# Fewer weight columns per level product, fixed PSUM tiles for the small products, and one instruction per sum of the state

## The chip, the cores and the metric

The kernel runs on 1 core of a Trainium2 chip. The metric is device time in microseconds (us): the median of the runs of one kernel. The kernel before took 584.26 us (median of 3 runs, 584.08 to 585.15).

## The reference, cut to what matters

An RWKV-6 recurrence (batch 4, 8 heads, 768 tokens, head dimension 48) feeds an expert layer of 2048 hidden units. Everything is fp32.

```python
for t in range(S):                       # S = 768
    cur   = einsum('bhd,bhe->bhde', u * k[t], v[t])
    y[t]  = einsum('bhd,bhde->bhe', r[t], state + cur)
    state = w[t][:, :, :, None] * state + einsum('bhd,bhe->bhde', k[t], v[t])
x = y.transpose(0, 2, 1, 3).reshape(3072, 384)
h = x @ w_in                             # 384 x 2048
g = h * erf(softplus(h))
out = g @ w_out                          # 2048 x 384
```

## The kernel before

**Steps.** The tokens are cut into 6 chunks of 128. A step `s` handles one chunk of two of the four batches, so there are 12 steps, 0 to 11. In a step stand 16 (batch, head) combinations, as 8 pairs `n` of two heads `e`. Head `e` of a pair has its 48 dimensions in partitions 64e to 64e+47 (`rows(e)`); partitions 48 to 63 and 112 to 127 are padding of zeros. A chunk is worked on as two halves of 64 tokens (`HC`).

**Level products.** Inside a half, what earlier tokens give to later ones is built up by levels 1 to 6. At level `l` the half is cut into blocks of 2^l tokens, and the later `half = 2^(l-1)` tokens of each block (queries r) meet its earlier `half` tokens (keys k). `level_products` (L540 to L556) does a level with 32 matmuls: for each pair, half and head, the key tokens are the weights (`lhsT`, one weight column per key token) and the query tokens of all right halves are the moving operand (32 columns; 64 at level 1). So the PSUM tile `pp` has key tokens in its partitions. `take_level` (L558) then copies from `pp` into `own` with `copy_predicated` (L562) only where a mask says that key and query belong to the two halves of one block. At levels 1 to 5 the weights are all 64 key tokens, at level 6 the first 32. Key tokens from 64 - `half` on lie in the last block's later half: no mask of levels 2 to 5 takes them. At level 1 the mask also holds the diagonal, so all 64 are needed there.

**Decay.** Between levels, `scale` (L328; L321 in step 0) multiplies the products of w into the tile `in` (r and k) in place, so a level waits for the `scale` of the level before, and that waits for the matmuls of its own level, which read `in`.

**Which levels run where.** Step 0 is `attend_first` (L746), steps 1 to 4 `attend` (L876), steps 5 to 11 `attend_late` (L693). Steps 0 to 3 run levels 1 to 6 on TensorE, step 4 levels 4 to 6, and steps 5 to 11 only levels 5 and 6: the nearer distances are there multiplied and summed up on VectorE and GpSimd (L453 to L484) and come back through DRAM as `by_tokens` (L514).

**State.** `state_part` (L650) multiplies keys and values of each half into PSUM, head 0 in partitions 0 to 47 and head 1 in 64 to 111. VectorE adds it to the faded state: `middle` after the first half (L736, L960, or a copy at L962), `S_next` after the second (L743, L965, L852); GpSimd fades `middle` in between (L739, L963). Each sum is a loop of two instructions, one for each head. `through_state` (L598, matmuls at L610) and `from_own` (L575, matmuls at L584) bring state and `own` into the output tile `y`.

**PSUM.** All small products share two tiles of 4 KB in each partition, `pp0` and `pp1`. Each call of `products` (L131) asks the pool for a new tile of that name, which may be used once everything that touched the one before it is released.

**The expert layer and the order.** `hidden` (L994, matmuls at L1027), `project` (L1044, L1059), `project_fast` (L1127, L1142) and `hidden_of_two` (L1210, L1230) do the two large products for earlier steps. The order on every engine is that of the code (a manual schedule): pieces of the expert layer are placed by hand between the levels (`place`, `beside`, and for the late steps lists of letters that `run_late` reads), so that TensorE has work while a level waits for VectorE. In step 0, where no such work exists yet, `keep_busy` (L867, matmuls at L871) and `stay_warm` (L858, matmuls at L862) put idle matmuls in the gaps. Steps 1 and 2 also turn the given weights into fp32 (L255 to L285).

The program names each matmul once; in the trace each fp32 matmul stands as two instructions, each with its own weight load, so that a level is 64 of them.

Of the kernel before, what the change touches and what calls it, by code (L numbers as in the profile page):

```python
# [11 lines left out]
FP32 = mybir.dt.float32  # L12
# [5 lines left out]
P = 128  # L18
FAST = 3
EP = 64  # L20
HC = 64
# [22 lines left out]
MASKED = 5  # L44
# [7 lines left out]
def rights(ap, half):  # L52

    names = "abcdefg"[: len(ap.shape) - 1]
    spread = " ".join(names)
    return ap.rearrange(f"{spread} (n two h) -> {spread} n two h", two=2, h=half)[
        (slice(None),) * len(names) + (slice(None), 1)
    ]
# [3 lines left out]
def kernel(  # L62
# [14 lines left out]
    nc = tc.nc  # L77
    PSUM = bass.MemoryType.PSUM

    n_steps, _, _, JP, C = rkw.shape  # L80
    NH, D = v.shape[2:]
    NP = JP // NJ
    NE = NH // JP
# [17 lines left out]
    ps_p = ctx.enter_context(tc.tile_pool(name="ps_p", bufs=1, space=PSUM))  # L101
# [7 lines left out]
    middle = const.tile([P, JP, D], FP32, name="middle")  # L109
    faded = [const.tile([P, JP, D], FP32, name="faded")] * NC  # L110
# [17 lines left out]

    turns = {"next": 0}

    def products(shape, n=None):  # L131


        if n is not None:
            return ps_p.tile(shape, FP32, name=f"pp{n}")
        n = turns["next"]
        turns["next"] = 1 - n
        return ps_p.tile(shape, FP32, name=f"pp{n}")

    loaded = {}  # L140

# [160 lines left out]

    def rows(e, n=D):
        return slice(e * EP, e * EP + n)

    def at(e, p):

        return rows(e ^ p & 1)
# [215 lines left out]
    def parts_of(s):  # L524

        c, i = divmod(s, SPC)
        in_t, vt = loaded[s]
        made, tots, tot = ready[s]
        ends = tot.rearrange("p (n h) -> p n h", h=NC)
        return c, in_t, vt, made, states[i][c % 2], states[i][1 - c % 2], ends  # L530

    def by_pair(t):

        return lambda x, n: t[:, x, n]
# [5 lines left out]
    def level_products(pp, rk, level, ns=range(NJ * NP)):  # L540

        half = 1 << (level - 1)
        m = HC if level <= MASKED else half
        for n in ns:
            for s0 in range(0, C, HC):
                for e in range(NE):
                    right = rk(0, n)[rows(e), s0 : s0 + HC]
                    to = pp[s0 : s0 + m, e, n, :]
                    if level > 1:
                        right = rights(right, half)  # L550
                        to = to[:, : HC // 2].rearrange("p (b h) -> p b h", h=half)
                    nc.tensor.matmul(  # L552
                        to, lhsT=rk(1, n)[rows(e), s0 : s0 + m], rhs=right,
                        start=True,
                        stop=True,
                    )  # L556

    def take_level(own, pp, level):  # L558
        half = 1 << (level - 1)
        got = pp[:].rearrange("p e n t -> p (e n) t")  # L560
        if level <= MASKED:
            nc.vector.copy_predicated(  # L562
                rights(own[:], half),
                rights(mask_sb[:, level - 1 : level, :].to_broadcast([P, NH, HC]), half),
                got[..., : HC // 2].rearrange("p n (b h) -> p n b h", h=half),
            )
        else:
            for s0 in range(0, C, HC):
                nc.scalar.copy(own[s0 : s0 + half, :, half:], got[s0 : s0 + half, :, :half])
# [5 lines left out]
    def from_own(s, own, swap):  # L575
        vt = loaded[s][1]
        for j in range(NJ):
            for q in range(0, NP, 2):
                for h in range(NC):
                    e = h ^ swap  # L580
                    for p in (q, q + 1):
                        n = j * NP + p
                        t = slice(h * HC, (h + 1) * HC)
                        nc.tensor.matmul(  # L584
                            y[at(e, p), e, p // 2, j, t],
                            lhsT=vt[t, n * NE + e, :], rhs=own[t, e * JP + n, :],
                            start=swap == 1 and not j and not q, stop=True,
                            skip_group_check=True,
                        )

    def fence():

        nc.vector.tensor_copy(
            out=seen[:].rearrange("p (e g t) -> p e g t", e=NE, g=NP),
            in_=y[:].rearrange("p e q j t -> p e (q j) t")[..., HC - 1 : HC + 1],
        )
# [96 lines left out]
    def attend_late(s, run):  # L693

        c, in_t, vt, own, S, S_next, ends = parts_of(s)
        RK = by_pair(in_t)
        before = s - 1 if s - 1 > DIRECT else None
        if before:
            from_own(before, ready[before][0], 1)
            fence()  # L700
        pp = products([P, NE, JP, HC], 0)
        level_products(pp, RK, LOG - 1)
        scale(s, LOG - 1)
        take_level(own, pp, LOG - 1)
        run("front", None)
        if before:
            from_own(before, ready[before][0], 0)
            through_state(before, xTs[before])
            if s + 1 < n_steps:
                load_step(s + 1)  # L710
        following = prepare(s + 1) if s + 1 < n_steps else iter(())
        next(following, None)
        nc.gpsimd.tensor_mul(faded[0][:], S[:], ends[:, :, 0:1].to_broadcast([P, JP, D]))
        next(following, None)
        run("near", None)
        next(following, None)
        kT = kTs[s]
        nc.vector.tensor_mul(
            kT[:].rearrange("p (e n) d -> p n e d", e=NE),
            kT[:].rearrange("p (e n) d -> p n e d", e=NE), spread[s][:],  # L720
        )
        run(0, following)

        pp = products([P, NE, JP, HC], 0)
        level_products(pp, RK, LOG)
        if s + 1 < n_steps:
            spread_blocks(s + 1, pp)
        take_level(own, pp, LOG)
        scale(s, LOG)
        run(1, following)  # L730
        ps = products([P, NC, JP, HC], 0)
        ps = [[ps[:, h]] * NE for h in range(NC)]
        state_part(s, kT, ps)
        run(2, following)
        for e in range(NE):
            nc.vector.tensor_add(middle[rows(e)], faded[0][rows(e)], ps[0][e][rows(e), :, :D])  # L736
        run(3, following)
        if s < n_steps - SPC:
            nc.gpsimd.tensor_mul(  # L739
                faded[1][:], middle[:], ends[:, :, 1:2].to_broadcast([P, JP, D])  # L740
            )
            for e in range(NE):
                nc.vector.tensor_add(S_next[rows(e)], faded[1][rows(e)], ps[1][e][rows(e), :, :D])  # L743
        run(4, following)

    def attend_first(xT):  # L746
# [5 lines left out]
        c, _, vt, made, S, S_next, ends = parts_of(0)  # L752
# [4 lines left out]
        pp = products([P, NE, JP, HC])  # L757
# [21 lines left out]
        for level in range(2, LOG):  # L779
            pp = turns.pop("pp", None) or products([P, NE, JP, HC])  # L780
# [21 lines left out]
        pp = turns.pop("pp")  # L802
# [29 lines left out]
        ps = [[products([P, NE, JP, HC], 1 - e)[:, e] for e in range(NE)]]  # L832
# [15 lines left out]
        def pending():  # L848
            part = products([P, NE, JP, HC], turns["next"])[:, 0]
            state_part(0, kT, ps + [[part] * NE], (1,))  # L850
            for e in range(NE):
                nc.vector.tensor_add(S_next[rows(e)], faded[1][rows(e)], part[rows(e), :, :D])  # L852
            load_third()
            stages["l"](5, S_next[:, 0, 0:1])

# [20 lines left out]
    def attend(s, xT, early, place, behind):  # L876

        c, in_t, vt, made, S, S_next, ends = parts_of(s)
# [9 lines left out]
        for level in range(near_log(s) + 1 if s == DIRECT else 1, LOG + 1):  # L888
            rk = by_pair(made) if level == 1 else RK
            pp = turns.pop("pp", None) or products([P, NE, JP, HC])  # L890
# [45 lines left out]
        ps = products([P, JP, P])  # L936
# [17 lines left out]
        ps = products([P, NC, JP, HC])  # L954
        ps = [[ps[:, h]] * NE for h in range(NC)]
        state_part(s, kT, ps)
        from_own(s, own, 0)
        for e in range(NE):
            if c:
                nc.vector.tensor_add(middle[rows(e)], faded[0][rows(e)], ps[0][e][rows(e), :, :D])  # L960
            else:
                nc.vector.tensor_copy(middle[rows(e)], ps[0][e][rows(e), :, :D])  # L962
        nc.gpsimd.tensor_mul(faded[1][:], middle[:], ends[:, :, 1:2].to_broadcast([P, JP, D]))  # L963
        for e in range(NE):
            nc.vector.tensor_add(S_next[rows(e)], faded[1][rows(e)], ps[1][e][rows(e), :, :D])  # L965
        for _ in following:
            pass
        place(LOG + 1)
# [433 lines left out]
    make_identity(nc, ident[:])  # L1402
    nc.vector.memset(y[:], 0.0)
    nc.vector.memset(sums[:], 0.0)
    apart = mixed[:].rearrange("p i f n -> p (i f n)")[:, : KT * P]
    apart = apart.rearrange("p (k m) -> p k m", k=KT)
    nc.vector.memset(apart, 0.0)
    for kk in range(KT):
        n = D // KT
# [187 lines left out]
```

## Time and profile before

| what | value |
|---|---|
| median of 3 runs | 584.26 us (584.08 to 585.15) |
| span of the profiled execution | 585.1 us, 0.84 above the median |
| granted TensorE clock, mean | 0.999 |
| TensorE matmuls (PE) busy | 576.4 us, 99% |
| weight loads (PEld) busy | 495.1 us, 85% |
| VectorE (DVE) busy | 454.7 us, 78%, 558 instructions |
| ScalarE (ACT), GpSimd (POOL) busy | 355.6 us, 274.1 us |
| L552, level products, weight loads of 64 columns, moving 32 | 1600 |
| L552, the same with weight loads of 32 columns (level 6) | 768 |
| L552, level 1, weight loads of 64 columns, moving 64 | 256 |
| sums of the state (L736, L743, L852, L960, L962, L965) | 42 instructions of 548 to 556 ns each |

How to read it: the span runs from the first to the last instruction of one execution on the chip. PE is busy while matmuls run, PEld while weights are loaded; the two overlap. A line like "x64" merges neighbouring instructions of one kind, and what stands in square brackets is how long the engine stood idle before them and what ended that. The chain of waits follows the work that ended last back to the start. The 1600 loads are 25 levels of 64: levels 2 to 5 in steps 0 to 3, levels 4 and 5 in step 4, level 5 in steps 5 to 11.

### The profile page before, as it was taken

The numbers are of one execution on the slowest core, as the hardware profiler recorded it, in microseconds if no ns is written. First come the engines' busy times: TensorE is split into PE (matmuls) and PEld (weight loads), VectorE is DVE, ScalarE is ACT, GpSimd is POOL, SyncE is SP. The second block draws the span as 40 slices with busy tenths as digits, with TensorE's granted clock in tenths as the row PEclk, the third lists the DMA queues.
The fourth block names the chain that finished last, engine by engine and source line by source line (L and its number), as shares of the span: only waits on it lengthen the run. The fifth ranks groups of instructions, "written<-read, shape, count | busy, mean of one in ns | idle before, by whom it ended". The sixth has DMA issues, their size and how long they took to land.

```text
span 585.1 us, 16663 instructions
## 1 busy us (share of the span) xinstructions
PE 576.4 (99%) x7240; PEld 495.1 (85%) x7240; DVE 454.7 (78%) x558; ACT 355.6 (61%) x478; POOL 274.1 (47%) x313
## 2 busy tenths in 40 slices
PE   8899999999999999999999999999999999999997
PEld 6588887688668758998898898898898899988997
DVE  6776886999996899799799799799799637256630
ACT  3658877644544598756766666665765771387700
POOL 4557391702398469659459459449549200000000
PEclk9999999999999999999999999999999999999999
DMA  8587571440433414334334334334331301000000
GB/s 269 177 273 281 201 235 44 183 154 10 145 95 116 117 55 156 63 116 165 74 111 169 74 108 172 75 108 136 74 108 55 74 8 36 2 0 2 28 27 29
DMA packets 54082, 63.25 MB, mean 108 GB/s; under 512 B 35160, under 2 KB 40568, under 8 KB 52984
## 3 DMA queue, kind: packets, MB, share of 16 engines
q1 hardware_dynamic: 53624, 61.98, 33.4%
q8 instruction: 57, 0.93, 0.6%
q10 hardware_dynamic: 384, 0.20, 0.1%
q14 instruction: 17, 0.14, 0.1%
HBM read 52.39 MB, written 8.69 MB: 104 GB/s over the span
## 4 chain that ended last, share of the span: by engine, by line
PE 95%; DVE 3%; issue 1%; ACT 0%; POOL 0%; DVEq 0%; POOLq 0%
PE m L1027 36%; PE m L1142 28%; PE m L1059 8%; PE pp L552 6%; PE pp L1230 4%; PE y L1230 2%; PE y L584 2%; PE pp L659 2%; PE y L610 2%; PE m L862 1%; PE pp L871 1%; PE pp L938 1%; DVE in L328 1%; DVE words L467 1%; PE pp L1142 0%
## 5 line engine op out<-in xcount | busy, mean ns | idle before, releaser
L1027 PE MATMUL m<-xT,w_in_sb 128*128 128x256 f32 x960 | 215.3, 382 | 0.1
L1027 PEld LDWEIGHTS m<-xT,w_in_sb 128*128 128x128 f32 x960 | 179.9, 190 | 26.2 <-issue 1.0
L328 DVE TENSOR_TENSOR in<-in,tot_sb 128x1024 f32<-128x1024 f32 (+1 forms) x55 | 75.3, 1369 | 16.5 <-PE pp L552 13.2
L463 POOL TENSOR_TENSOR rk<-words 128x528 f32<-128x528 f32 (+3 forms) x28 | 42.5, 1517 | 91.2 <-DVE sums L453 80.7
L1036 ACT COPY h<-m 128x512 f32<-128x512 f32 x80 | 46.4, 579 | 57.6 <-PE m L1027 57.5
L467 POOL TENSOR_TENSOR words<-words,rest 128x528 f32<-128x528 f32 (+10 forms) x77 | 78.1, 1015 | 6.0
L1059 PE MATMUL m<-w_out_sb,h 128*128 128x384 f32 x192 | 64.3, 491 | 0.0
L1059 PEld LDWEIGHTS m<-w_out_sb,h 128*128 128x128 f32 x192 | 35.7, 190 | 23.5
L1142 PE MATMUL m<-mixed,h 128*128 128x192 f32 x256 | 45.6, 331 | 0.0
L1142 PE MATMUL m<-w_out_sb,h 128*128 128x192 f32 x256 | 44.8, 329 | 0.0
L552 PEld LDWEIGHTS pp<-in 48*64 48x64 f32 (+1 forms) x2368 | 33.4, 126 | 12.0 <-issue 6.2
L1142 PEld LDWEIGHTS m<-mixed,h 128*128 128x128 f32 x256 | 41.4, 190 | 0.9
L1142 PEld LDWEIGHTS m<-w_out_sb,h 128*128 128x128 f32 x256 | 41.6, 190 | 0.3
L1142 PE MATMUL m<-w_out_sb,room 128*128 128x192 f32 x240 | 41.5, 326 | 0.0
L983 ACT ACT_TABLE_LOAD x30 | 38.5, 1283 | 2.7 <-issue 2.2
L987 ACT ACT_TABLE_LOAD x30 | 38.5, 1283 | 1.5 <-DVE room L1125 1.1
L1142 PEld LDWEIGHTS m<-w_out_sb,room 128*128 128x128 f32 x240 | 39.4, 190 | 0.0
L402 POOL TENSOR_TENSOR tot_sb<-tot_sb 128x256 f32<-128x256 f32 (+4 forms) x50 | 36.2, 724 | 3.8
L552 PE MATMUL pp<-in 48*64 48x32 f32 (+1 forms) x2368 | 37.3, 212 | 0.6 <-DVE in L328 0.5
L463 POOL TENSOR_TENSOR words<-words 128x336 f32<-128x336 f32 (+6 forms) x49 | 35.3, 720 | 3.8
L453 DVE TENSOR_REDUCE sums<-rk 128x14 f32<-128x672 f32 (+9 forms) x54 | 34.7, 701 | 0.0
L453 DVE TENSOR_REDUCE sums<-words 128x6 f32<-128x288 f32 (+8 forms) x66 | 26.9, 464 | 3.9 <-POOL words L463 3.6
(198 smaller groups left out, 951.5 us busy)
## 6 DMA issues: line engine op xcount, KB each, us to landing
in<-in_rkw SPq DMA_DIRECT2D x8, 1024.0 KB, 5.1
words<-in_moe_w_in SPq DMA_DIRECT2D x16, 384.0 KB, 5.4
words<-in_moe_w_out SPq DMA_DIRECT2D x16, 384.0 KB, 4.7
words<-in_rk_rows SPq DMA_DIRECT2D x8, 768.0 KB, 5.6
w<-in_rkw SPq DMA_DIRECT2D x11, 512.0 KB
v<-in_v SPq DMA_DIRECT2D x12, 384.0 KB, 5.6
out<-o SPq DMA_DIRECT2D x23, 192.0 KB, 2.4
in<-in_rkw SPq DMA_DIRECT2D x7, 512.0 KB, 5.7
```

Source lines behind the costliest of these rows:

```text
L328: nc.vector.tensor_mul(halves, halves, view(tots[level - 1], 0, [[1, n], [2, nb], [0, half]]))
L402: nc.gpsimd.tensor_mul(new, pair[:, :, 0], pair[:, :, 1])
L453: nc.vector.tensor_reduce(out=view(sums[:], n, [[near * (NEAR + 1), NEAR // near], [NEAR + 1, near - n]]), in_=terms[n], axis=mybir.AxisLi ...
L463: engine.tensor_mul(terms[n], r[:, :, n:], k[:, :, : near - n])
L467: engine.tensor_mul(k[:, :, :m], k[:, :, :m], w[:, :, n : n + m])
L552: nc.tensor.matmul(to, lhsT=rk(1, n)[rows(e), s0 : s0 + m], rhs=right, start=True, stop=True,)
L983: nc.scalar.activation(sp_room, chunks[0], AF.Softplus)
L987: nc.scalar.activation(at, sp_room, AF.Erf)
L1027: nc.tensor.matmul(ps[:, ff, :], lhsT=w_in_sb[:, g * FG + f + ff, kk * P : (kk + 1) * P], rhs=xT[:, kk, :], start=kk == 0, stop=kk == KT - 1,)
L1036: nc.scalar.copy(h[:, f : f + FT, :], ps[:])
L1059: nc.tensor.matmul(ps[j][:], lhsT=gs[g][:, f, j * C : (j + 1) * C], rhs=w_out_sb[:, g * FG + f, :], start=g + f == 0, stop=g == NG - 1 and ...
L1142: nc.tensor.matmul(to, lhsT=a[:, f], rhs=b[:, f], start=start and f == 0, stop=f == FG - 1, skip_group_check=True,)
```

## The change

Three edits, none of which moves an instruction to another place in the order.

1. At levels 2 to 5 the weights are the first 64 - `half` key tokens: 62, 60, 56 and 48 columns at levels 2, 3, 4 and 5. Level 1 keeps 64, level 6 keeps 32.
2. `products` no longer asks the pool: two tiles `banks` are taken once, set to zero by VectorE at the start (two memsets of 128x1024), and every product is a view of one of them. The rows that a level now leaves unwritten keep what was there.
3. Each sum of the state is one instruction over partitions 0 to 111 (`both`) in place of two over 48 partitions each; the padding in between is summed with it and never read.

```diff
+    banks = [ps_p.tile([P, NE * JP * HC], FP32, name=f"pp{n}") for n in range(2)]
+
     def products(shape, n=None):
-        if n is not None:
-            return ps_p.tile(shape, FP32, name=f"pp{n}")
-        n = turns["next"]
-        turns["next"] = 1 - n
-        return ps_p.tile(shape, FP32, name=f"pp{n}")
+        if n is None:
+            n = turns["next"]
+            turns["next"] = 1 - n
+        names = "abc"[: len(shape) - 1]
+        return banks[n][:].rearrange(
+            f"p ({' '.join(names)}) -> p {' '.join(names)}", **dict(zip(names, shape[1:]))
+        )
...
+    both = slice(0, EP + D)
...
     def level_products(pp, rk, level, ns=range(NJ * NP)):
         half = 1 << (level - 1)
-        m = HC if level <= MASKED else half
+        m = HC - half if 1 < level <= MASKED else HC if level == 1 else half
...
     # attend_late; the same in attend (with the copy at its first chunk) and in pending()
-        for e in range(NE):
-            nc.vector.tensor_add(middle[rows(e)], faded[0][rows(e)], ps[0][e][rows(e), :, :D])
+        nc.vector.tensor_add(middle[both], faded[0][both], ps[0][0][both, :, :D])
...
-            for e in range(NE):
-                nc.vector.tensor_add(S_next[rows(e)], faded[1][rows(e)], ps[1][e][rows(e), :, :D])
+            nc.vector.tensor_add(S_next[both], faded[1][both], ps[1][0][both, :, :D])
...
     nc.vector.memset(sums[:], 0.0)
+    for t in banks:
+        nc.vector.memset(t[:], 0.0)
```

More of the change, by code (lines that the diff above doesn't have):

```diff
@@ L850, in pending @@
             state_part(0, kT, ps + [[part] * NE], (1,))
-            for e in range(NE):
-                nc.vector.tensor_add(S_next[rows(e)], faded[1][rows(e)], part[rows(e), :, :D])
+            nc.vector.tensor_add(S_next[both], faded[1][both], part[both, :, :D])
             load_third()
@@ L957, in attend @@
         from_own(s, own, 0)
[L958 to L962, printed above, removed]
+        if c:
+            nc.vector.tensor_add(middle[both], faded[0][both], ps[0][0][both, :, :D])
+        else:
+            nc.vector.tensor_copy(middle[both], ps[0][0][both, :, :D])
         nc.gpsimd.tensor_mul(faded[1][:], middle[:], ends[:, :, 1:2].to_broadcast([P, JP, D]))
-        for e in range(NE):
-            nc.vector.tensor_add(S_next[rows(e)], faded[1][rows(e)], ps[1][e][rows(e), :, :D])
+        nc.vector.tensor_add(S_next[both], faded[1][both], ps[1][0][both, :, :D])
         for _ in following:
```

## The prediction

> **What bounds the kernel now.** I read the engines' busy time first, then the chain of waits by engine:
>
> ```profile
> PE 576.4 (99%) x7240; PEld 495.1 (85%) x7240; DVE 454.7 (78%) x558; ACT 355.6 (61%) x478; POOL 274.1 (47%) x313
> ...
> PE 95%; DVE 3%; issue 1%; ACT 0%; POOL 0%; DVEq 0%; POOLq 0%
> ```
>
> TensorE is on 95% of the chain. A busy PE need not be a late one, so I looked next at the waits of PE over the whole span:
>
> ```profile
> PE pp L552 <- issue: 1.3, 1, 1.3
> PE pp L659 <- issue: 0.9, 1, 0.9
> PE pp L871 <- DVE own L562: 0.7, 2, 0.4
> PE pp L552 <- DVE in L328: 0.5, 1, 0.5
> ```
>
> Columns: total us, times, longest. Beside these PE waits only at the start (1.7 us for `ident`) and 0.2 us at L610. All lie before 29.9 us except the last line, 0.54 us at 165.06 in step 4; in the windows 29.9 to 120.7, 165.06 to 241 and 241 to 502.4 us PE is busy 90.72 of 90.81, 75.94 of 75.94 and 261.40 of 261.40 us. So from step 1 on, time is what TensorE's own stream takes: a shorter run of matmuls brings the end nearer by what it saves, and VectorE's relief brings nothing except at 165.06.
>
> What a level costs TensorE is in the timeline of step 3 and 4:
>
> ```profile
> 60.09 1.03 PEld L552 LDWEIGHTS pp<-rk 48*64 48x64 f32 x64
> ...
> 119.57 1.02 PEld L552 LDWEIGHTS pp<-in 48*64 48x64 f32 x64 [0.55 <-DVE in L328]
> ...
> 126.01 0.65 PEld L552 LDWEIGHTS pp<-in 48*32 48x32 f32 x64 [0.33 <-DVE in L328]
> ...
> 138.87 0.81 PEld L659 LDWEIGHTS pp<-v,kT 64*48 64x48 f32 x64 [0.33 <-issue]
> 139.59 0.52 PEld L584 LDWEIGHTS y<-own,v 64*48 64x48 f32 x32
> ```
>
> and in the chain, in order of time:
>
> ```profile
> 119.64 1.06 PE pp L552 x64
> ...
> 126.08 0.69 PE pp L552 x50
> ...
> 132.15 0.59 PE y L584 x32
> ...
> 138.94 0.87 PE pp L659 x64
> ```
>
> (The 0.69 us hold all 64 of level 6; the chain lists 50 of them.) Runs of 64: 64 weight columns and 32 moving take 1.06 us, 32 and 32 take 0.69, 48 and 48 take 0.87. Level 1 (first line of the timeline, in step 2), with 64 moving columns in place of 32, loads in 1.03, as level 5 does with 32. With 64 weight columns the moving operand is therefore not the limit; weight columns are, and 48 are not charged as 64.
>
> **The level products.** Price of one column, off every instruction of a run of 64: from 64 and 32 columns (1.06 - 0.69)/32 = 0.0116 us; from 64 and 48, (1.06 - 0.87)/16 = 0.0119; from the loads alone, (1.02 - 0.81)/16 = 0.0131. I take 0.0118. Level 5 loses 16 columns (0.19 us), level 4 loses 8 (0.094), level 3 loses 4 (0.047), level 2 loses 2 (0.024).
>
> Steps 1 to 3 run all four levels: 3 x 30 = 90 columns. Step 4 runs levels 4 and 5: 24. Steps 5 to 11 run level 5: 7 x 16 = 112. Together 226 columns x 0.0118 = **2.67 us**, all in stretches where PE has no gap.
>
> Widths 62, 60 and 56 occur nowhere in the trace. Bounds: if they are charged as 64, only level 5 counts, 11 x 16 x 0.0118 = 2.08; with the loads' price everything, 226 x 0.0131 = 2.96. I take the straight line, since 32, 48 and 64 lie on it within 0.01 us.
>
> Step 0 I cost at nothing, though it loses 30 columns (0.35 us). VectorE is the limit there:
>
> ```profile
> 14.99 0.69 DVE L562 COPY_PREDICATED own<-mask_sb,pp 128x512 f32<-128x512 int32 x1
> ...
> 15.71 1.29 DVE L321 TENSOR_TENSOR in<-in,tot_sb 128x512 f32<-128x512 f32 x2
> ...
> 16.92 0.71 DVE L562 COPY_PREDICATED own<-mask_sb,pp 128x512 f32<-128x512 int32 x1
> ```
>
> One level goes round in 1.93 us of VectorE without a gap, and PE's 0.84 us of `keep_busy` fill the rest. Ends: 0 and 0.35.
>
> A rule of the Trainium skill bears on the price. "TensorE: Matmul & The Clock Gate", section "LDWEIGHTS (loading the stationary operand)", gives a load as its columns divided by 1.2 in ns; as an estimate from that page, with loads one after another, 226 x 64 x 0.833 ns would be 12 us. The same page, section "Wait — 56ns, not 53.3ns?", speaks against the change: start to start never falls below about 25 ns however small the matmul, so that nothing would be gained. Here 64 instructions in 0.69 us are 10.8 ns apart, and in 1.06 us 16.6 ns: both below that floor, and still moving with the columns, so the row decides.
>
> **The sums of the state.** 42 instructions of about 0.55 us become 21. The 48x384 rows and ScalarE's and VectorE's 128x384 copies (L821: 0.556 us over 128 partitions) say that the columns set the time, not the partitions, so each pair saves 0.55, or 11.6 us of VectorE in all. It lies beside TensorE's work everywhere but at one place:
>
> ```profile
> 141.41 1.13 DVE L960 TENSOR_TENSOR middle<-faded,pp 48x384 f32<-48x384 f32 x2
> ...
> 143.56 1.12 DVE L965 TENSOR_TENSOR s<-faded,pp 48x384 f32<-48x384 f32 x2 [1.01 <-POOL faded L963]
> ...
> 165.06 0.76 PE L552 MATMUL pp<-in 48*32 48x32 f32 x64 [0.54 <-DVE in L328]
> ```
>
> From 143.56 to 165.0 VectorE has no gap, and the last of it is the `scale` that level 6 of step 4 waits for. Both sums shorten (the second starts earlier too, as GpSimd's fade follows the first): VectorE is 1.1 us earlier there. TensorE's own saving by then (90 + 24 columns, 1.35 us) makes it arrive earlier as well; but VectorE's chain hangs on TensorE's level 3 of step 3 (wait at 107.92), so it also gains what is saved up to there (0.85). VectorE 1.1 + 0.85 = 1.95 earlier against PE's 1.35: of the 0.54 us wait about 0.6 is covered, so it goes: **0.5 us**. If VectorE were not relieved, the wait would grow to about 1.0. What is late next is TensorE itself.
>
> **The fixed tiles.** Two memsets of 128x1024 join VectorE's start, each like `y`'s:
>
> ```profile
> 1.02 0.91 DVE L1403 MEMSET y<- 128x1024 f32 x1 [1.02 <-PEq L1585]
> ...
> 5.10 0.42 DVE L372 TENSOR_TENSOR rk<-in,u_sb 128x256 f32<-128x256 f32 x1 [2.44 <-DMA u_sb<-in_u]
> ```
>
> They take 1.87 us of the 2.44 that VectorE waits for the first DMA: cost nothing, 0.57 left. Without that cover each us would delay step 0. The built order shows the rest: the same matmuls, DMAs, SP and GpSimd instructions in the same order, some twenty waits of TensorE on itself dropped (each for matmuls long done, and PE shows no wait at those places), and a few waits added. VectorE's sums of steps 1 to 3 also wait for ScalarE, whose `kT` copy ended at 134.6 before the sum at 141.41; behind them on VectorE stand `scale` and L514, and nobody gains or loses. ScalarE's first `few` (L678, 166.12) also waits for VectorE, whose reading of that tile had to end before the matmuls that it copies; behind it stand the copies of level 6. Two L1027 in steps 1 and 2 name TensorE itself, for pieces finished a level earlier. Value 0; ends -0.3 and +0.5.
>
> **Sum.** 2.67 + 0.5 = 3.2 us: from the span of 585.1 to 581.9, and as the profiled execution lies 0.84 above the median of the shown runs, 584.26 to **581.1**.
>
> **Rivals.** (a) *Half of it*: only width 48 pays (2.1), or step 1's levels 2 to 5, where VectorE's `scale` ends within 0.15 us of the level (41.26 against 41.40, 45.27 against 45.32), give theirs back (0.35), or the 0.5 at 165.06 stays: 581.6 to 583.0. For it: unseen widths; against: the line through three widths, and VectorE's own 0.55 at L852 ahead of those levels. (b) *More*: the loads' price, and step 0's 0.35 as well: 2.96 + 0.5 + 0.35, to 580.4; and if the two stalls marked "issue" (0.9 at 22.9, 1.3 at 28.1) fall more kindly, to 579.5. (c) *Nothing*: the run is set by the number of instructions once loads are shorter, or those stalls grow by 2 to 3 us; 583.1 to 585.4. Against: level 6 has as many instructions and needs 0.69. (d) *Slower*: 48-column loads go at the pace of L584, which has 48 columns and needs 0.59 for 32, so 1.18 for 64, 0.12 more than 64 columns in L552. Over the 21 runs of steps 1 to 11 that is +2.5, less 0.5: 586.3. It decides from 1.084 us a run (0.5/21 above 1.06). For it: also 48 columns; against: L584 moves 64 columns, L659 with 48 needs 0.87, and L552 moves 32. (e) *VectorE was the limit*: its 11.6 us would show, 573; PE without a gap from 165 to 502 us excludes it.
>
> **How the numbers follow.** Forecast 580.5 to 582.0: 0.60. (a) beyond that: 0.17. (b) beyond that: 0.08. (c) 0.09, (d) 0.06, (e) nil. The range 579.8 to 583.0 holds the forecast, (a) and half of (b): 0.81. A measurement of this kernel tells 0.2% (1.2 us) from no change: faster 0.85, same 0.09, slower 0.06.
>
> **What would show it.** After: level 5's 64 loads in 0.81 to 0.85 us and its chain pieces at 0.87 or less; level 4 near 0.96; level 2 barely under 1.06. No PE wait at step 4's level 6, or under 0.2. VectorE busy some 10 us less (11.6 less 1.8), with PE at 573 to 574 busy. Steps 6 to 10 each about 0.19 us shorter. Wrong if level 5's run stays at 1.06 or grows, or if PE shows new waits for VectorE in steps 1 to 3, or longer "issue" stalls before 30 us.

## The result, and the profile after

The changed kernel took 581.49 us (median of 15 runs), the kernel before, beside it, 584.52: a ratio of 0.9956, with a 95% interval of 0.9943 to 0.9969. A second set of runs gave 0.9947 (0.9927 to 0.9967). So it is faster by 2.6 to 3.1 us by the two ratios (the medians of the first set lie 3.0 apart); 581.1 was predicted, 3.2 less than before. Lines of the kernel have moved: the level products are L557 now (L552 before), `scale` is L333 (L328), the products with `own` are L589 (L584).

The page of the profile after, engines and chain, answers to the first lines shown of before:

```profile
PE 573.2 (99%) x7240; PEld 491.9 (85%) x7240; DVE 443.9 (76%) x539; ACT 354.9 (61%) x478; POOL 277.9 (48%) x313
...
PE 92%; DVE 4%; POOL 1%; DMA 1%; issue 1%; ACT 0%; SPq 0%; DVEq 0%; POOLq 0%; ACTq 0%
```

TensorE is 3.2 us less busy, VectorE 10.8. TensorE's share of the chain fell from 95 to 92%: other engines now end some waits. The longest waits of PE after, but for that at the start (total us, times, longest):

```profile
PE pp L557 <- DVE in L333: 1.1, 2, 0.8
PE pp L873 <- DVE own L567: 0.6, 2, 0.4
```

The two stalls marked "issue" are not there, and there is a new wait of 0.8 us for VectorE's `scale` (L333 now), at level 5 of step 1. The weight loads of step 2, one line for each of levels 2 to 6:

```profile
60.93 1.00 PEld L557 LDWEIGHTS pp<-in 48*62 48x62 f32 x64 [0.33 <-DVE own L917]
...
67.51 0.97 PEld L557 LDWEIGHTS pp<-in 48*60 48x60 f32 x64 [0.33 <-issue]
...
71.31 0.92 PEld L557 LDWEIGHTS pp<-in 48*56 48x56 f32 x64 [0.33 <-issue]
...
75.06 0.81 PEld L557 LDWEIGHTS pp<-in 48*48 48x48 f32 x64 [0.33 <-issue]
...
78.70 0.65 PEld L557 LDWEIGHTS pp<-in 48*32 48x32 f32 x64 [0.33 <-issue]
```

With 64 columns each of the first four was 1.02. In the chain the runs are spaced 1.04, 1.01, 0.96 and 0.85 us in place of 1.06: the price goes by the column, also between 56 and 64. And level 6 of step 4, where PE had stood idle 0.54 us:

```profile
161.62 0.76 PE L557 MATMUL pp<-in 48*32 48x32 f32 x64
```

No bracket: the wait is gone.

**Where the time went.** The steps by the timelines, each from the first matmul of its level products (step 1: of the expert layer) to that of the next; two profiled executions of each kernel:

| stage, us | before | after | difference of means | predicted |
|---|---|---|---|---|
| start to first L1027 | 29.89, 29.89 | 27.86, 28.26 | -1.83 | 0 |
| step 1 | 30.26, 30.19 | 30.53, 30.10 | +0.09 | -0.35 |
| step 2 | 33.75, 33.98 | 33.05, 33.03 | -0.83 | -0.35 |
| step 3 | 52.60, 52.60 | 52.54, 52.60 | -0.03 | -0.35 |
| step 4 | 49.64, 49.27 | 48.72, 48.71 | -0.74 | -0.3 - 0.5 |
| step 5 | 45.32, 46.25 | 45.68, 45.66 | -0.12 | -0.19 |
| steps 6 to 10 | 222.74, 222.49 | 221.49, 221.48 | -1.13 | -0.95 |
| step 11 to the end | 120.90, 120.93 | 120.73, 120.66 | -0.22 | -0.19 |
| span | 585.1, 585.6 | 580.6, 580.5 | -4.8 | -3.2 |

The spans differ by more than the times because both profiled executions of before lay above their medians: a run's time is 1.8 us above its span (582.34 for the span of 580.6), so the span of 585.1 stands for some 586.9, 2.6 above the first median of before, and that of 585.6 was a run of 587.38, 2.2 above the median of its set. From step 2 on the profiles differ by 3.1 us; what the spans differ by beyond that lies in the first 30 us.

### The profile page after: what moved, and what is told of

The parts are those of the page before. It is cut to its first block, busy times and chain, and to the rows that moved or that the text cites. A ratio compares the mean times of both kernels' runs of the same rounds, so it can differ in the third digit from the quotient of the medians.

```text
span 580.6 us, 16629 instructions
## 1 busy us (share of the span) xinstructions
PE 573.2 (99%) x7240; PEld 491.9 (85%) x7240; DVE 443.9 (76%) x539; ACT 354.9 (61%) x478; POOL 277.9 (48%) x313
## 4 chain that ended last, share of the span: by engine, by line
PE 92%; DVE 4%; POOL 1%; DMA 1%; issue 1%; ACT 0%; SPq 0%; DVEq 0%; POOLq 0%; ACTq 0%
PE m L1027 34%; PE m L1142 28%; PE m L1059 9%; PE pp L557 5%; PE pp L1230 4%; PE y L1230 2%; PE y L589 2%; PE y L615 2%; PE pp L664 2%; PE m L864 1%; DMA words<-in_moe_w_in 1%; DVE in L333 1%; PE pp L873 1%; PE pp L940 1%; DVE rk L468 1%
## 5 line engine op out<-in xcount | busy, mean ns | idle before, releaser
L1027 PE MATMUL m<-xT,w_in_sb 128*128 128x256 f32 x960 | 215.2, 382 | 0.0
L1027 PEld LDWEIGHTS m<-xT,w_in_sb 128*128 128x128 f32 x960 | 179.9, 190 | 25.8 <-ACT h L1036 1.0
L333 DVE TENSOR_TENSOR in<-in,tot_sb 128x1024 f32<-128x1024 f32 (+1 forms) x55 | 75.2, 1367 | 14.1 <-PE pp L557 11.8
L1036 ACT COPY h<-m 128x512 f32<-128x512 f32 x80 | 46.3, 581 | 59.0 <-PE m L1027 58.9
L557 PEld LDWEIGHTS pp<-in 48*48 48x48 f32 (+4 forms) x2368 | 30.1, 120 | 12.8 <-issue 5.6
L557 PE MATMUL pp<-in 48*48 48x32 f32 (+4 forms) x2368 | 33.9, 206 | 1.2 <-DVE in L333 1.1
L407 POOL TENSOR_TENSOR tot_sb<-tot_sb 128x256 f32<-128x256 f32 (+4 forms) x50 | 32.6, 652 | 3.8
```

The lines of the kernel that those rows point to most:

```text
L333: nc.vector.tensor_mul(halves, halves, view(tots[level - 1], 0, [[1, n], [2, nb], [0, half]]))
L557: nc.tensor.matmul(to, lhsT=rk(1, n)[rows(e), s0 : s0 + m], rhs=right, start=True, stop=True,)
L1027: nc.tensor.matmul(ps[:, ff, :], lhsT=w_in_sb[:, g * FG + f + ff, kk * P : (kk + 1) * P], rhs=xT[:, kk, :], start=kk == 0, stop=kk == KT - 1,)
L1036: nc.scalar.copy(h[:, f : f + FT, :], ps[:])
```

## The experiments

The theory (A): TensorE's stream is the limit, and the gain is its shorter weight loads. Rivals: the fixed tiles' dropped waits (B) or their memsets (C), VectorE's relief (D), and next limits that take part of the saving back (E, and what followed). Ratios are to the kernel before, with 95% intervals:

| kernel | ratio | interval |
|---|---|---|
| `banks`: fixed tiles alone | 1.0016 | 0.9999 to 1.0032 |
| `cols`: tiles and columns | 0.9979 | 0.9962 to 0.9996 |
| `sums`: tiles and single sums | 1.0004 | 0.9991 to 1.0018 |
| the change, again | 0.9947 | 0.9927 to 0.9967 |
| `thin`: 32 columns at levels 2 to 5 | 0.9927 | 0.9911 to 0.9944 |
| before, again | 1.0007 | 0.9987 to 1.0027 |
| `relief` | 0.9945 | 0.9926 to 0.9963 |
| `order1` | 0.9982 | 0.9962 to 1.0002 |
| `order3` | 0.9946 | 0.9927 to 0.9964 |
| `orders` | 1.0000 | 0.9984 to 1.0015 |

**The three edits apart.** `banks` undoes columns and sums, `cols` only the sums, `sums` only the columns:

```diff
-        m = HC - half if 1 < level <= MASKED else HC if level == 1 else half   # banks, sums
+        m = HC if level <= MASKED else half
...
-        nc.vector.tensor_add(middle[both], faded[0][both], ps[0][0][both, :, :D])   # banks, cols
+        for e in range(NE):
+            nc.vector.tensor_add(middle[rows(e)], faded[0][rows(e)], ps[0][e][rows(e), :, :D])
...                                                # the other sums alike
```

> The fixed tiles and their two memsets alone: 64 weight columns at levels 2 to 5, two instructions for each sum, as before. Theory A (the gain is TensorE's shorter weight loads): same as before within 0.5 us, level 5 at 1.06 us a run, PE wait of about 0.5 us at step 4's level 6. Rival B (the dropped waits of TensorE on itself are part of the gain): 0.5 to 2 us faster than before. Rival C (the memsets cost time at the start): up to 0.5 us slower, with the first product of VectorE later than 5.1 us.

> Fixed tiles and fewer weight columns, but two instructions for each sum of the state. Theory A: 2.67 us of columns less about 0.5 us of longer wait at step 4's level 6 (from 0.54 to about 1.0), so some 2.2 us faster than before, ratio 0.996; the change as a whole gave 0.9956. Rival D (the gain is VectorE's relief): within 1 us of before.

> Fixed tiles and one instruction for each sum, but 64 weight columns as before. Theory A: VectorE is busy some 10 us less, and the kernel only 0.5 us faster than before, by the wait at step 4's level 6, which goes from 0.54 to 0; PE busy unchanged at 576. Rival D: 2 us faster or more.

Fixed tiles alone bring nothing (B falls), and may cost up to 0.3%; in `banks` VectorE's first product came at 5.14 us in place of 5.10, so C is not shown either. Sums alone bring nothing that can be told. Columns alone bring 0.21% against before (1.2 us, where 2.2 were expected) and 0.37% against `banks` (2.2 us); the whole change brings 0.44 to 0.53%. Which of the two is the columns' share hangs on the cost of the fixed tiles, which the intervals leave open. What joins columns and sums is level 6 of step 4, here in `banks`, `cols` and `sums`, in this order:

```profile
164.75 0.76 PE L557 MATMUL pp<-in 48*32 48x32 f32 x64 [0.69 <-DVE in L333]
```

```profile
163.13 0.76 PE L557 MATMUL pp<-in 48*32 48x32 f32 x64 [1.12 <-DVE in L333]
```

```profile
162.41 0.76 PE L557 MATMUL pp<-in 48*32 48x32 f32 x64
```

Columns alone make TensorE arrive earlier and wait longer, and step 4 takes 49.91 us in `cols` against 49.79 in `banks`. Sums alone take the wait away (49.04). Together 48.72. D falls: of VectorE's 10.8 us no more is seen to count than this wait, 0.75 us without and 1.2 with the shorter loads. The wait itself varies: 0.54 and 0.17 us in the two profiles of before, 0.69 in `banks`.

**More of the same.** `thin` has 32 columns at levels 2 to 5:

```diff
-        m = HC - half if 1 < level <= MASKED else HC if level == 1 else half
+        m = HC if level == 1 else HC // 2
```

> As the change, but 32 weight columns at all of levels 2 to 5, which leaves out the products of half of the key tokens there (it shows only the time). Each run at levels 2 to 5 then costs 0.69 us as level 6 does. Against the change this takes off 294 columns in steps 1 to 3, 40 in step 4 and 112 in steps 5 to 11. Theory A with TensorE as the limit everywhere: 446 x 0.0118 = 5.3 us faster than the change. Theory E (in steps 1 to 3 the next engine is already level with TensorE, so that more saving there comes back as waits): only steps 4 to 11 pay, 152 x 0.0118 = 1.8 us faster than the change, with PE waits for VectorE in steps 1 to 3 growing to about 3 us.

The ratio is 0.9927, 1.7 us below the change's 0.9956 and 1.2 below its 0.9947: near E's 1.8 in the total, but not by its own account. Steps 6 to 10 take 221.38 us against 221.49: there 16 columns of level 5 brought 0.1 us in five steps, where A and E both have 0.9. The weight loads and matmuls of a late step, in the change

```profile
326.50 0.66 PE L589 MATMUL y<-own,v 64*48 64x64 f32 x32
326.93 0.83 PEld L557 LDWEIGHTS pp<-in 48*48 48x48 f32 x64
326.98 0.89 PE L557 MATMUL pp<-in 48*48 48x32 f32 x64
```

and in `thin`:

```profile
280.30 0.66 PE L589 MATMUL y<-own,v 64*48 64x64 f32 x32
280.89 0.65 PEld L557 LDWEIGHTS pp<-in 48*32 48x32 f32 x64
280.89 0.76 PE L557 MATMUL pp<-in 48*32 48x32 f32 x64
```

With 48 columns level 5 begins to load 0.43 us after L589 starts, between L589's last matmuls; with 32 columns 0.59 us after, when all of L589's have started. In the chain the runs take 0.71 and 0.69 us: what the narrower loads save, the lost overlap costs. Before the change, with 64 columns, this run took 0.91 us in the chain against 1.06 elsewhere, so that the overlap of some 0.15 us was there too. The Trainium skill has a rule that fits ("TensorEngine Tiling (Array Packing)", "Key Properties"): changing the tiling mode, and not only the tile, drains the engine. L589 loads 48 columns, as level 5 does after the change; that 32 columns are another mode, and 48 and 64 the same, is a guess. The lost overlap agrees with it; no run measured a drain by itself.

In steps 1 to 3 `thin` saved 98 columns a step, 1.16 us by the price, and got 0.78, 0.35 and 0.08 us of it against the change's first profile, with PE waits of 1.0 us for VectorE in step 1 and 1.0 for GpSimd's conversion of `w_out` (L288) in step 3. So other engines do stand right behind TensorE there.

**Once more, side by side.** Both kernels unchanged:

> The kernel before, unchanged, profiled once more. It tells what of the differences in the first 60 us is the change's. Theory F (the two stalls of TensorE marked issue, 2.1 us between 22 and 30 us, are an accident of that one execution, of DMA traffic): they are gone or elsewhere, first matmul of the expert layer near 27.5 us in place of 29.9. Theory G (the fixed tiles took them away): they are there again, at 29.9. Ratio 1.000 within the interval.

> The change, unchanged, profiled once more beside the other kernels of this call. Theory A: ratio 0.995 to 0.997, step 3 again near 52.5 us and steps 6 to 10 at 44.30 us each. The PE wait of 0.84 us at step 1's level 5 comes back only if it is systematic (VectorE's scale behind a load of weights); if it is an accident of DMA, it is elsewhere or gone.

The waits of PE in the second profile of before:

```profile
PE pp L552 <- issue: 1.3, 1, 1.3
PE pp L659 <- issue: 1.2, 1, 1.2
```

The same stalls at the same places, so F falls as put: in both profiled executions of before they are there. They lie 256 TensorE instructions apart (128 pairs of load and matmul). The queue for instructions moves 57 packets of 16 KB in all, and TensorE's 14480 loads and matmuls over 57 are 254 a packet. The packets' own times in the traces fit: those of before landed at 22.54 and 27.91 us, and TensorE went on at 23.81 and 29.40; in the second profile they landed at 22.36 and 28.10, and it went on at 23.80 and 29.40. In all 13 profiles the stalls marked "issue" end 1.3 to 1.6 us after such a packet landed, and none of the blocks of 256 in the first 42 us begins sooner than 1.27 us after its packet. So TensorE waits there for its next instructions; no run changed anything about that by itself.

G holds only in part. `banks`, `cols`, `relief` and `orders` have no such stall over 0.15 us, `sums` and `thin` one of 0.2 us. But the second profile of the change has 0.4 and 0.7 us in the same places, `order3` and `moving` have 0.7 in the second, and `order1` has 0.4 one block earlier. And `banks`, 2.4 us earlier at its first matmul of the expert layer, lost 1.8 of it in step 1, which took 32.01, with waits of 0.6 and 0.8 us for VectorE's `scale`.

That wait for the `scale` at level 5 of step 1 came again in the second profile of the change, with 0.42 us. It does not come from shorter loads: `banks` and `sums`, with 64 columns, have 0.84 and 0.56 us there.

**What takes the saving of step 3 back.** `relief` leaves out near products of VectorE, those of distances 4 to 7:

```diff
-            term(nc.vector, 3, 4, 5, 6, 7)
+            term(nc.vector, 3)
             nc.vector.tensor_mul(terms[0], terms[0], r)
             yield
-            sum_up(*range(near))
+            sum_up(*range(4))
```

`order3` moves those of distances 5 to 7 behind the `scale` that level 6 waits for (each `yield` hands over to the next place in the step):

```diff
-            term(nc.vector, 3, 4, 5, 6, 7)
+            term(nc.vector, 3, 4)
+            yield
+            term(nc.vector, 5, 6, 7)
             nc.vector.tensor_mul(terms[0], terms[0], r)
-            yield
             sum_up(*range(near))
```

> The change with VectorE relieved in step 3: the near products at distances 4 to 7 that VectorE prepares there for step 4 are left out, and their sums (their share of the output is missing, which shows only the time). That takes about 2.7 us of VectorE out of the stretch between levels 4 and 6 of step 3. Theory E (in step 3 VectorE is level with TensorE and takes the saving back): step 3 falls from 52.54 us to about 52.2, which is 52.60 less 0.36 of columns, and the PE wait of 0.28 us at its level 6 goes; other steps as in the change. Rival H (step 3 did not shorten for another reason, such as ScalarE's copies that free the PSUM tiles of the expert layer): step 3 stays at 52.5.

> The change, with VectorE's near products of distances 5 to 7 (for step 4) moved behind the scale that level 6 of step 3 waits for; nothing is left out. Theory E: the PE wait at level 6 of step 3 (0.28 us by the profile, 0.36 to 0.40 by the spacing of the runs) goes, step 3 falls from 52.54 and 52.60 to 52.2 us, all else as in the change; 0.4 us faster than the change, which the times alone can hardly tell. Rival K (with VectorE out of the way, GpSimd's conversion of w_out holds TensorE, as it did by 0.6 us in the run with less work for VectorE): step 3 stays at 52.6 with a PE wait at L1059.

In the change, VectorE's `scale` and level 6 of step 3 (the first line is VectorE's):

```profile
122.23 1.22 DVE L333 TENSOR_TENSOR in<-in,tot_sb 128x1024 f32<-128x1024 f32 x1
```

```profile
123.50 0.69 PE L557 MATMUL pp<-in 48*32 48x32 f32 x58 [0.28 <-DVE in L333]
```

The runs up to there are 0.39 us shorter, and the expert layer's piece before level 6 occupies 5.73 us instead of 5.38: 0.36 us given back at one wait. In `relief` that piece is 5.38 again, so E is right about this wait. But step 3 stayed at 52.80, because one piece earlier another engine was late:

```profile
115.56 4.14 PE L1059 MATMUL m<-w_out_sb,h 128*128 128x384 f32 x12 [0.34 <-POOL w_out_sb L288]
```

`order3` shows the same (0.17 us, and step 3 at 52.63): K. `moving`, below, waits there too, 0.35 us, with VectorE's work as in the change. In `orders`, below, neither wait occurred:

```profile
114.14 5.43 PE L1060 MATMUL m<-w_out_sb,h 128*128 128x384 f32 x16
119.50 0.92 PE L558 MATMUL pp<-in 48*48 48x32 f32 x64
120.35 5.45 PE L1028 MATMUL m<-xT,w_in_sb 128*128 128x256 f32 x24
125.73 0.76 PE L558 MATMUL pp<-in 48*32 48x32 f32 x64
```

and step 3 took 52.19 us, 0.4 below before, as the columns say. But `order1` and `cols`, without the new order of `order3`, took 52.38 and 52.31, with waits of 0.12 and 0.04 us at level 6. So two engines stand close behind TensorE in step 3, and which is last, and by how much, changes between executions; that the new order by itself brings step 3 down is not shown. H is not needed.

**Step 1.** `order1` puts VectorE's `scale` ahead of the shift of the weights; `orders` has that and `order3`:

```diff
+            scale(s, level)
             if s == 1 and 2 < level:
                 stages["h"](level + 1)
-            scale(s, level)
```

> The change, with VectorE's scale ahead of the shift of the weights (L275) at levels 3 to 6 of step 1, so that the scale no longer stands behind a shift that waits for a load of weights. Theory I (step 1's PE waits for VectorE, 0.84, 0.4 and 1.5 us in three executions of the change or of a kernel like it up to there, come from that load): no PE wait for the scale in step 1, which takes 29.7 us (30.1 less about 0.4) in place of 30.5, 30.1 and 33.0; the kernel 0.4 to 1 us faster than the change. Rival J (the load is late whatever the order, and the next product of the expert layer waits for its weights instead): step 1 as long as before, with PE waits at L1027 for GpSimd.

> Both orders together. Theories E and I: 0.8 to 1.4 us faster than the change, ratio to before 0.993 to 0.994, span near 579.7. Rivals J and K: as the change, 0.995.

Theory I falls. Step 1 took 32.04 and 33.77 us, the kernels were 2 to 3 us slower than the change. J as put is not seen either: PE has no wait for GpSimd at L1027. The wait for the `scale` shrank to 0.2 us, but a new one came, in `order1` (total us, times, longest):

```profile
PE y L589 <- ACT h L1036: 1.9, 1, 1.9
```

The view names ScalarE's L1036, but that copy ended at 51.43 us. What ended just before L589's first load was VectorE's last shift:

```profile
48.40 2.82 DVE L333 TENSOR_TENSOR in<-in,tot_sb 128x1024 f32<-128x1024 f32 x1 [0.25 <-POOL block_sb L910]
51.14 0.95 DVE L275 TENSOR_SCALAR w_in_sb<-y 128x768 int32<-128x768 int32 x1
```

```profile
52.15 0.54 PEld L589 LDWEIGHTS y<-own,v 64*48 64x48 f32 x32 [2.32 <-ACT h L1036]
```

The shift reads `y`, which holds a part of the weights there, and L589 writes `y`; TensorE's wait ahead of L589 names VectorE's semaphore among two and ended at 52.13, 0.05 us after the shift. In the change the shift ran at 47.63, ahead of the `scale`. So the new order put what L589 waits for behind a `scale` of 2.82 us.

In `orders` the same wait comes, and another thing: TensorE's granted clock is 0.5 for 3.4 us from 52.7 us on (0.59 in the mean of 52 to 56), which is 1.7 us of its 33.77. `relief`, which has the change's step 1, had that too, from 42.1 us, so that its step 1 took 32.97. Both came soon after a wait of TensorE of 1.5 to 1.9 us; but `order1` has the same wait at full clock, so no rule follows from it.

And the `scale` itself became slower. VectorE and GpSimd in `order1`:

```profile
39.82 1.82 POOL L288 TENSOR_TENSOR w_in_sb<-w_in_sb,rest 128x768 int32<-128x768 int32 x1 [0.77 <-DVE w_in_sb L275]
40.19 2.53 DVE L333 TENSOR_TENSOR in<-in,tot_sb 128x1024 f32<-128x1024 f32 x1
```

In the change the same `scale`, there at 42.51 us and alone, took 1.22 us. The Trainium skill ("SBUF — State Buffer", "Terms") has VectorE and GpSimd hold a shared port pair for a whole instruction, with the loser blocked. That agrees within 0.14 us: L288 ends at 41.64, 1.45 after the `scale` began, and 1.45 + 1.22 is 2.67 against the 2.53 measured. Where L288 began after the `scale`, as in step 2 of the change (64.39 and 64.62 us), the `scale` took 1.22 and L288 2.68 in place of 1.82.

**What sets the pace of a run.** `moving` gives levels 2 to 5 all 64 query tokens as the moving operand:

```diff
-                    if level > 1:
+                    if level > MASKED:
                         right = rights(right, half)
```

> The change with 64 moving columns at levels 2 to 5 in place of 32 (all query tokens instead of the right halves; what is taken from PSUM is then wrong, the time is what it is for). Rule 1 (a run goes at the pace of the longer of its two operands, weight columns or moving columns, at 0.25 ns a column and instruction): every run at levels 2 to 5 takes 1.04 to 1.06 us again, also level 5 with 48 weight columns, as L584's runs do (0.52 us for 32 loads), and the kernel is 2 to 3 us slower than the change. Rule 2 (weight columns alone set the pace): level 5 stays at 0.85 us and the time at that of the change.

A single execution took 585.03 us, so that of the times only the order of size can be used. Its chain at level 5 of step 3 and of step 4:

```profile
118.27 1.04 PE pp L557 x64
...
154.11 1.04 PE pp L557 x64
```

With 48 weight columns and 64 moving columns the run is back at 1.04 us, from 0.85, and steps 6 to 10 take 222.43 us in place of 221.48: rule 1. It also explains why L584 (L589 now), with 48 weight columns, is no faster: it moves 64. The 0.25 ns a column fit 64 columns (16.6 ns an instruction) and not 32 (10.8 ns).

## Why the prediction was right, and where it was not

- **The columns' price** held: 0.85, 0.96, 1.01 and 1.04 us a run, against 0.87, 0.97, 1.01 and 1.04 by the straight line. By these runs the 226 columns came to 2.9 us where 2.67 were summed. Rival (a)'s first part, that only width 48 pays, is out, and so is (d): by `moving`, L584's pace comes from its moving operand.
- **Steps 4 to 11** came as summed: 0.3 + 0.5 in step 4 (0.74 measured), 0.19 a step after that (0.20 in each of steps 7 to 10, 44.50 to 44.30). Without the relief of VectorE the wait at 165.06 was to grow to 1.0; `cols` has 1.12. Part of that is luck, as the wait of 0.54 us was that of one execution (0.17 in the second profile of before). And one term was added up wrongly: the saving up to level 3 of step 3 is 66 columns, 0.78 us and not 0.85, so that the lead of VectorE covers the wait only just, and without the relief 1.1 would have been left, as `cols` shows. That a sum over 112 partitions takes no longer than one over 48 held: 543 to 558 ns after, 548 to 556 before.
- **Steps 1 to 3** were the step that failed in part: "all in stretches where PE has no gap". The runs there are 0.39 us a step shorter, 1.17 in all. Step 3 gave 0.36 back to VectorE's chain, which the prediction had left out among the rivals though it lists step 1's. Step 1 shows no gain, as rival (a) feared, and it has the wait for VectorE's `scale` (0.84 and 0.42 us); but `banks` and `sums` have that with 64 columns, so it comes from TensorE's earlier arrival or the fixed tiles, and which is not shown. New waits for VectorE in steps 1 to 3 were the prediction's own sign of being wrong, and they came. Step 2 shows 0.83 less, but kernels with the same step 2 took 33.03 to 33.95 us, so no more than its 0.39 can be put down to the change.
- **Step 0 and the start** were costed at nothing. In the profiled executions they are 1.8 us shorter, mostly by stalls that the prediction had only in rivals (b) and (c). The times do not show that gain in full (2.6 to 3.1 against 4.8 in the spans), and why is not settled: the stalls are seen only where an execution was profiled. That the total came so near 3.2 is therefore in part luck: some 0.8 us of steps 1 and 3 did not come, the columns gave 0.2 more, and how much of the start is in the times is not known.
- **The time** was subtracted from a median, which was right; that the profiled execution lay "0.84 above" it was wrong, as its time is 1.8 above its span. As only the difference of 3.2 was taken off the median, the forecast did not move.
- **VectorE's memsets** cost nothing measurable at the start: the gap before its first product absorbed them (5.11 us in place of 5.10).

What stays open: why TensorE's instructions come later in the profiled executions of before than in most others, and which part of the first 60 us the change owns. `banks` at 1.0016 leaves room for a small cost of the fixed tiles. No version tried beats the change: `order3` equals it, and `thin` and `relief` leave work out.

## What to carry to other kernels

For a run of small matmuls, compare runs of different weight widths and moving widths in the trace first: here the longer of the two operands set the pace, and cutting it paid column by column, until with 32 columns a lost overlap with the run before it took the rest. Where TensorE is busy without a gap, ask at each later wait how much room the next engine has; here the 0.39 us saved in step 3 came through wholly, in part or not at all, and relief of VectorE, worth nothing that can be told alone, was worth 1.2 us in step 4 beside shorter loads. Check the end of the engine that a view names for a wait: where it ended long before, look for another. And compare stages of several executions, with their granted clock, before the spans: the first 60 us of the same code took 58.4 us in the change and 60.3 in `relief`, 1.7 of it by the clock.

## What the runs showed of the hardware that had not been expected

- A run of matmuls 48 rows deep goes at the longer of weight columns and moving columns, as far as these four show: 48 and 32 take 0.85 us for 64 instructions, 64 and 32 take 1.06, 48 and 64 take 1.04, 32 and 32 take 0.69.
- Level 5 with 48 columns overlaps the end of L589's run before it (0.71 us in the chain for 64), with 32 columns it does not (0.69): a third fewer columns brought 0.02 us. With 64 it did (0.91 against 1.06).
- VectorE's 128x1024 product took 1.22 us alone, and 2.5 to 2.8 us in `order1` where it began while GpSimd's addition L288 ran; where the addition began second, it was the addition that took longer (2.68 in place of 1.82).
- TensorE stalled 0.2 to 1.3 us at blocks of 256 of its instructions, always until 1.3 to 1.6 us after a 16 KB packet of the instruction queue had landed.
- In two of the profiles (`relief`, `orders`) TensorE was granted half its clock for 3.4 us in the midst of the span, which cost 1.7 us each.
